# Threshold attention and hash routing: quarter products and sums in PSUM for the experts

## The chip, the cores and the metric

The kernel runs on one core of a Trainium2 chip. Its metric is the device time of one launch in microseconds. Five engines work from queues of their own: TensorE (PE, with its weight loads listed as PEld), VectorE (DVE), ScalarE (ACT), GpSimd (POOL) and SyncE (SP, which only issues DMAs here). All matrices are float32. SBUF holds 128 partitions; PSUM, into which TensorE writes, is used here as tiles of 128 x 2 x 512 floats.

## The reference

```
scores = q @ k^T / sqrt(64)               # 8 batches x 8 heads, 576 x 576
scores = where(scores >= rowmax - tau, scores, -1e9)
attn   = softmax(scores) @ v              # 8 x 8 x 576 x 64
x      = attn as rows                     # 4608 tokens x 512
expert = token_id * 2654435761 % 8        # one of 8 for each token
out    = relu(x @ w1[expert]) @ w2[expert]     # w1 512 x 1024, w2 1024 x 512
```

## The kernel before, in words

The first 500 us or so are attention: pairs of heads, one after the other, with the routing (each token's slot among the tokens of its expert) worked out beside it and the rows of x scattered to DRAM. The change does not touch that part. Around 500 us it goes over into the expert part; everything below is about that.

**Experts.** The experts are sorted by size and get room for 544 tokens (e = 0), 576 (e = 1 to 4) and 600 (e = 5 to 7). Tokens stand along the free axis: x^T is held as 128 x 4 x tokens (`xT_bufs`, two of them), h as 128 x 8 x tokens (`h_0`), the result as 128 x 4 x tokens (`oT`). Layer 1 is h = relu(w1^T x^T), layer 2 is oT = w2^T h. Each is cut into 2 x 2 blocks: the weight's a11, a12, a21, a22 and the tokens' b11, b12, b21, b22, each with half the contraction and half the outputs or half the tokens.

**Seven products.** `seven` (L926) multiplies the blocks with Winograd's form of Strassen's method, seven products for eight. In the product's notation, with sums s1 to s4 of a and t1 to t4 of b (`left` L863, `right` L869; four DVE adds each, in `sums_w1`, `sums_x`, `sums_w2`, `sums_h`):

```
p1 = a11 b11;   u2 = p1 + s2 t2;   u3 = u2 + s3 t3;   u4 = u2 + s1 t1
c11 = p1 + a12 b21;   c21 = u3 + a22 t4;   c22 = u3 + s1 t1;   c12 = u4 + s4 b22
```

Every product is an accumulation of its own in one of four PSUM tiles, taken in turn by `bank2` (L851) from two pools of two. ACT copies p1 into SBUF (L951); DVE makes u2, u3, u4 in SBUF (`halves`) and c11 to c22 (adds, L861; subtractions L858). In layer 1 ACT then applies the ReLU in place (L948). Layer 1 runs in two groups g of 256 outputs each, a product being 2 x 2 calls of matmul (L941); layer 2 is one group with 2 x 4 calls. A call is as wide as half the tokens: 272, 288 or 300 columns, and 240 in layer 2 of e = 7, whose last 120 tokens are done by `last_tile` (L983). The weights of w2 are read with a stride of four columns ("dealt"), except for e = 7. Layer 1 of expert 0 is done as plain products, in part during attention (`early_h`, `late_h`, L632 and L652, with `fill` placing matmuls in gaps).

**Order.** Nothing here is planned by a scheduler. The order of the calls in the code (`manual_schedule`, L1069 to L1122) is the order in each engine's queue, and each engine runs its queue in order; semaphores make it wait for others. The side work of an expert is handed out after each product by `side1` (in layer 1) and `side2` (in layer 2):

- `sums_w2(e)`, `sums_h(e)` in layer 1; `sums_w1(e+1)`, `sums_x(e+1)` in layer 2, on DVE;
- `put_squares(e, i)` (L1024): DVE transposes oT by squares of 32 x 32 into `o_q`, then POOL writes 10 (i = 0, step 3 of layer 2) or 9 (i = 1, step 0 of the next expert) blocks of rows to `out` by indirect DMA;
- `fetch(e+2)` (L1045, step 2 of layer 2): five indirect DMAs on POOL bring rows of x into `xg`;
- `turn_x(e+1)` (L1052): five DVE transposes xg into `xq` (in layer 1, steps 3 to 5), then `move`: 16 DMAs issued by SP, xq into the other xT;
- `load_w1(e+2)` (step 4 of layer 2) and `load_w2(e+2)` (after it): 2 MB each, issued by SP, into a pool of two buffers each.

The end is `put_out` (L997: PE transposes, copies, row writes of the last expert) and `last_tile`.

Of the kernel before, what the change touches and what calls it, by code (L numbers as in the profile page):

```python
# [20 lines left out]
def kernel(  # L21
# [94 lines left out]
    w_tiles = {}  # L116
# [15 lines left out]
    def load_w1(e):  # L132
        w1_sb = w_pool.tile([P, CO, F], FP32, name="w1_sb")
        nc.sync.dma_start(out=w1_sb[:],
                          in_=w1[bass.ds(expert_at(e), 1)].rearrange("o (c p) f -> p (o c) f", p=P))
        w_tiles[e, 1] = w1_sb
# [690 lines left out]
    with tc.tile_pool(name="m_x", bufs=1) as m_x, \  # L827
         tc.tile_pool(name="m_o", bufs=3) as m_o, \
# [9 lines left out]
        o_end = m_x.tile([P, DIN], FP32, name="o_end")  # L838
        mark = m_x.tile([P, 1], FP32, name="mark")
        w1_s = m_s.tile([P, 3, C2, F2], FP32, name="w1_s")  # L840
        CH = CAP // 2
        x_s = m_s.tile([P, 3, C2, CH], FP32, name="x_s")
        w2_s = m_s.tile([P, 3, FH, D2], FP32, name="w2_s")
        h_s = m_s.tile([P, 3, FH, CH], FP32, name="h_s")
        halves = [m_s.tile([P, 2, CH], FP32, name=n) for n in ("p1", "u2", "u3", "u4")]
# [3 lines left out]
        turn = [0]  # L849

        def bank2():  # L851
            turn[0] ^= 1
            if turn[0]:
                return ps_sc.tile([P, 2, 512], FP32, name="sc")
            return ps_m.tile([P, 2, 512], FP32, name="bank2")
# [31 lines left out]
        def w2_sums(e):  # L887
            t = triple(w2_s, 0, FH)
            return t if e == E - 1 else [dealt(x, C2) for x in t]
# [19 lines left out]
        def sums_w2(e):  # L909
            s1 = None  # L910
            if e == E - 1:
                spare = w_pool.tile([P, CO, F], FP32, name="w1_sb")
                s1 = w_tiles["s1"] = spare[:, :, 0:D2]
            return left(*w2_blocks(e, w_tiles[e, 2]), w2_sums(e), s1)
# [11 lines left out]
        def seven(a, a_s, b, b_s, m0, outs, relu, after):  # L926

            (a11, a12, s1, a22), (s2, s3, s4) = a, a_s
            (b11, t1, b21, b22), (t2, t3, t4) = b, b_s
            c11, c12, c21, c22 = outs  # L930
            n_k, width, dealt_out = a11.shape[1], b11.shape[2], len(a11.shape) == 4
            p1, u2, u3, u4 = (t[:, :, 0:width] for t in halves)

            def product(x, y):
                ps = bank2()
                for i in range(2):
                    c0 = m0 + P * i
                    for c in range(n_k):
                        lhsT = (x[:, c, :, i] if dealt_out else
                                x[:, c, c0:c0 + P])  # L940
                        nc.tensor.matmul(ps[:, i, 0:width], lhsT=lhsT, rhs=y[:, c],  # L941
                                         start=c == 0, stop=c == n_k - 1)
                return ps[:, :, 0:width]

            def out(c, ps, u, step):
                add(c, ps, u)()
                if relu:
                    nc.scalar.activation(c, c, AF.Relu)  # L948
                after(step)

            nc.scalar.copy(p1, product(a11, b11))  # L951
            out(c11, product(a12, b21), p1, 0)
            add(u2, product(s2, t2), p1)()
            after(1)
            add(u3, product(s3, t3), u2)()
            after(2)
            out(c21, product(a22, t4), u3, 3)
            k5 = product(s1, t1)
            add(u4, k5, u2)()
            out(c22, k5, u3, 4)  # L960
            out(c12, product(s4, b22), u4, 5)

        def layer1(e, side):

            w, half = w_tiles.pop((e, 1)), caps[e] // 2
            for g in range(NG):
                outs = [h_0[:, FH * i + 2 * g:FH * i + 2 * g + 2, half * k:half * k + half]
                        for i in range(2) for k in range(2)]
                seven(w1_blocks(w), triple(w1_s, 0, C2), x_blocks(e), triple(x_s, 0, C2, half), 2 * P * g,
                      outs, True, lambda step: side(g, step))  # L970

        def layer2(e, side):
# [5 lines left out]
            if e == E - 1:  # L978
                a[2] = w_tiles["s1"]
            seven(a, w2_sums(e), h_blocks(0, FH, half),  # L980
                  triple(h_s, 0, FH, half), 0, outs, False, side)

        def last_tile(middle):  # L983

            w, o_sb, idx = w_tiles[E - 1, 2], o_end, gidx[:, KT - 1:KT]
# [11 lines left out]
        def put_out(e, *groups):  # L997
# [14 lines left out]
            for tr, kts in zip(trs, groups):  # L1012
                for i, kt in enumerate(kts):
                    rows = rows_of(kt)
                    o_sb = m_o.tile([P, DIN], FP32, name="o_sb")
# [53 lines left out]
        with tc.manual_schedule():  # L1069
            run(sums_w2(0), 4)  # L1070
            fill(18)
            late_h(lambda fo: (ps_sc.tile([P, 2, 512], FP32, name="sc") if fo in (2, 4) else
                               ps_m.tile([P, 2, 512], FP32, name="bank2")))
# [3 lines left out]
        with tc.manual_schedule():  # L1077
            for e in range(E):
# [3 lines left out]
                if e > 0:  # L1082
                    w2_work, h_work = sums_w2(e), sums_h(e, 0, 2)

                    def side1(g, step):
                        if g == 0:
                            run(w2_work)
                            if step == 0:
                                put_squares(e - 1, 1)
                        else:  # L1090
                            run(h_work)
                        if step > 2:
                            run(turns, 1 if g == 0 else 2)
# [3 lines left out]
                x_work = (sums_w1(e + 1) + sums_x(e + 1)) if more else []  # L1097

                def side2(step):
                    if step == 0:  # L1100
                        run(turns, len(turns))
                    else:
                        run(x_work, 2)
# [4 lines left out]
                    if more and step == 3:  # L1108
# [88 lines left out]
```

## Time and profile before

| | |
|---|---|
| device time, three runs | 931.68, 934.79, 939.22 us (median 934.79) |
| the profiled execution's own time | 931.3 us |
| its span | 929.7 us |
| granted TensorE clock, mean | 0.996 |
| PE busy | 909.8 us (98%) |
| PEld busy | 662.0 us |
| DVE busy | 757.5 us (81%) |
| ACT busy | 457.3 us |
| POOL busy | 403.7 us |

The profile is one execution on the chip. A busy time counts the time in which an engine had an instruction running; waits and the issue of DMAs are not in it. Weight loads of TensorE are listed apart, since they run beside its matmuls. Lines of the timeline give the start and length in us, the engine, the line of the code, the operation, output<-inputs by the program's names, the shape and how many instructions in a row; what stands in brackets is the idle time before and what ended it. Lines of the waits give the waiting engine's output and line, whom it waited for, the sum in us, how often, and the longest.

### The profile page before, as it was taken

To read this page: it belongs to the slowest core of one execution; us is meant where nothing else is said; L and a number is where in the kernel's file an instruction comes from. 1 tells how busy PE (TensorE), PEld (TensorE's weight loads), DVE (VectorE), ACT (ScalarE), POOL (GpSimd) and SP (SyncE) were. 2 spreads that over 40 slices of the span, in tenths; PEclk is the share of its full clock that TensorE was granted. 3 is DMA by queue.
4 is the path that set the end of the run, shared out by engine and by line. 5 is a ranking of instruction groups with operands and counts; after the bars stand their busy time and mean duration, and the time that the engine had idled before them with its cause. 6 is when DMAs were issued, how large, how long until landed. Compare 5 with 4: busy or idle time off the path is not lost.

```text
span 929.7 us, 20725 instructions
## 1 busy us (share of the span) xinstructions
PE 909.8 (98%) x7495; PEld 662.0 (71%) x7495; DVE 757.5 (81%) x1654; ACT 457.3 (49%) x741; POOL 403.7 (43%) x528
## 2 busy tenths in 40 slices
PE   7999999999999999999999999999999999999996
PEld 4666666656666566665678888788887978878785
DVE  7999999999999999999955776767668676777551
ACT  6888888888888898888812010110201021020110
POOL 4232432456666623455423370724527073440702
PEclk9999999999999999999999999999999999999999
DMA  7354463554545668743101745364372536412101
GB/s 175 92 148 118 109 152 93 136 131 103 123 105 153 159 165 214 216 107 88 30 25 51 237 131 158 133 173 141 95 223 75 164 133 165 157 34 50 48 3 55
DMA packets 114775, 113.11 MB, mean 122 GB/s; under 512 B 32475, under 2 KB 89315, under 8 KB 114672
## 3 DMA queue, kind: packets, MB, share of 16 engines
q1 hardware_dynamic: 105168, 92.64, 37.0%
q0 software_dynamic: 9072, 18.91, 7.0%
q8 instruction: 61, 1.00, 0.4%
q14 instruction: 42, 0.34, 0.1%
q10 hardware_dynamic: 432, 0.21, 0.1%
HBM read 81.99 MB, written 21.44 MB: 111 GB/s over the span
## 4 chain that ended last, share of the span: by engine, by line
PE 65%; issue 21%; POOL 7%; DVE 3%; ACT 2%; DMA 1%; another core or an unknown queue 1%; POOLq 0%; SPq 0%; DVEq 0%; ACTq 0%
PE av L313 18%; PE sc L235 15%; PE tr L282 11%; PE sc L941 9%; PE bank L941 8%; POOL out_dram L1036 6%; PE sc L640 2%; PE av L282 1%; POOL xg L119 1%; ACT w L260 1%; DVE ns L246 1%; DVE w L271 1%; ACT wT_b L303 1%; ACT wT_a L303 0%
## 5 line engine op out<-in xcount | busy, mean ns | idle before, releaser
L260 ACT ACTIVATE w<-ns,nmx 128x576 f32<-128x576 f32 x288 | 220.5, 777 | 28.8 <-DVE ns L246 27.8
L271 DVE SCALAR_TENSOR_TENSOR w<-ns,thr,w 128x576 f32<-128x576 f32 x288 | 225.8, 816 | 0.0
L1036 POOL DMA_INDIRECT out_dram<-o_q,qidx x127 | 138.1, 1087 | 191.7 <-DVE o_q L1028 153.1
L246 DVE TENSOR_SCALAR_CACHE_REDUCE ns<-sc 128x576 f32<-128x576 f32 x288 | 205.6, 747 | 8.1 <-PE sc L235 7.4
L253 POOL TENSOR_SCALAR thr<-nmx,drop 128x2 f32<-128x2 f32 (+1 forms) x160 | 104.4, 653 | 187.3 <-DVE ns L246 177.6
L235 PE MATMUL sc<-k_sb,q 64*128 64x288 f32 (+1 forms) x1280 | 179.2, 423 | 1.0 <-DVE drop L704 0.7
L282 PEld LDWEIGHTS tr<-ident,w 64*128 64x128 f32 x2624 | 106.0, 138 | 95.4 <-ACT wT_b L303 32.4
L282 PE MATMUL tr<-ident,w 64*128 64x64 f32 x2624 | 139.5, 231 | 6.0 <-ACT wT_b L303 2.6
L948 ACT ACTIVATE h<-h 128x576 f32<-128x576 f32 (+1 forms) x56 | 38.7, 693 | 164.8 <-DVE h L861 126.1
L235 PEld LDWEIGHTS sc<-k_sb,q 64*128 64x128 f32 (+1 forms) x1280 | 93.0, 177 | 23.2 <-DVE ns L246 9.4
L313 PE MATMUL av<-wT_a,v 128*64 128x320 f32 (+1 forms) x704 | 100.6, 418 | 0.2
L303 ACT COPY wT_a<-tr 128x512 f32<-128x512 f32 (+1 forms) x128 | 81.7, 638 | 20.7 <-PE tr L282 20.2
L303 ACT COPY wT_b<-tr 128x512 f32<-128x512 f32 (+1 forms) x128 | 81.4, 636 | 17.1 <-PE tr L282 11.2
L313 PE MATMUL av<-wT_b,v 128*64 128x256 f32 x640 | 83.2, 389 | 0.0
L313 PEld LDWEIGHTS av<-wT_a,v 128*64 128x64 f32 x704 | 43.8, 137 | 29.3 <-DVE xm L352 0.7
L951 ACT COPY p<-bank 128x576 f32<-128x576 f32 (+2 forms) x11 | 7.0, 633 | 99.5 <-PE bank L941 72.5
L313 PEld LDWEIGHTS av<-wT_b,v 128*64 128x64 f32 x640 | 40.2, 136 | 18.8 <-issue 0.7
L542 POOL DMA_INDIRECT slot_scratch<-tok,slot_i x36 | 45.0, 1251 | 9.4 <-issue 7.6
L941 PE MATMUL bank<-h,w_sb 128*128 128x288 f32 (+3 forms) x192 | 48.1, 404 | 0.0
L941 PE MATMUL sc<-h,w_sb 128*128 128x288 f32 (+3 forms) x192 | 47.7, 401 | 0.0
L941 PEld LDWEIGHTS bank<-h,w_sb 128*128 128x128 f32 x192 | 46.6, 300 | 0.5
L941 PEld LDWEIGHTS sc<-h,w_sb 128*128 128x128 f32 x192 | 45.9, 289 | 0.6
(197 smaller groups left out, 1303.7 us busy)
## 6 DMA issues: line engine op xcount, KB each, us to landing
w_sb<-in_moe_w_dram SPq DMA_DIRECT2D x16, 2048.0 KB
q<-in_q_dram SPq DMA_DIRECT2D x62, 288.0 KB
v<-in_v_dram SPq DMA_DIRECT2D x32, 256.0 KB
x_scratch<-xm SPq DMA_DIRECT2D x32, 256.0 KB
xT<-xq SPq DMA_DIRECT2D x84, 80.0 KB
k_sb<-in_k_dram SPq DMA_DIRECT2D x31, 144.0 KB
k_sb<-in_k_dram SPq DMA_DIRECT2D x32, 112.0 KB
x_scratch<-xg SPq DMA_DIRECT2D x9, 256.0 KB
```

What stands on the lines that cost most here:

```text
L235: nc.tensor.matmul(sc[out_rows, i, 0:S2], lhsT=q_sb[rows, h, q0:q1], rhs=k_sb[rows, h], start=True, stop=True)
L246: nc.vector.tensor_scalar(out=ns[:].rearrange("p (i s) -> p i s", i=2), in0=sc[:, :, 0:S2], scalar1=-1.0, scalar2=None, op0=ALU.mult, op1= ...
L253: nc.gpsimd.tensor_scalar(out=thr[:, 0:j + 1], in0=stats[n][0][:, 0:j + 1], scalar1=drop[:], scalar2=None, op0=ALU.add)
L260: nc.scalar.activation(w, nss[n, j][:], AF.Exp, bias=stats[n][0][:, j:j + 1], scale=-1.0)
L271: nc.vector.scalar_tensor_tensor(out=w, in0=nss.pop((n, j))[:], scalar=stats[n][1][:, j:j + 1], in1=w, op0=ALU.is_le, op1=ALU.mult, accum_ ...
L282: nc.tensor.transpose(dst[:, r, 64 * c:64 * c + 64], src[rows, c0:c0 + P], ident[rows, rows])
L303: nc.scalar.copy(dst, tr[:, :, 0:64 * n_c].rearrange("p r (c q) -> p r c q", c=n_c))
L313: nc.tensor.matmul(av[64 * j:64 * j + 64, g, c0:c1], lhsT=v_sb[:, c, 64 * j:64 * j + 64], rhs=wT[g][:, i, c0:c1], start=(c == 0), stop=stop)
L542: nc.gpsimd.indirect_dma_start(out=slot_dram[c % 2][:, :], out_offset=bass.IndirectOffsetOnAxis(ap=slot_i[:, c:c + 1], axis=0), in_=tok[:, ...
L941: nc.tensor.matmul(ps[:, i, 0:width], lhsT=lhsT, rhs=y[:, c], start=c == 0, stop=c == n_k - 1)
L948: nc.scalar.activation(c, c, AF.Relu)
L1036: inst = nc.gpsimd.indirect_dma_start(out=rows[:, :], out_offset=bass.IndirectOffsetOnAxis(ap=idx, axis=0), in_=o_sb, in_offset=None, boun ...
```

## The change

Two things are done, and the side work is dealt out anew.

**Sums in PSUM.** `seven` becomes the class `Seven`. p1 stays in its PSUM tile and s2 t2, s3 t3 and a22 t4 are accumulated on top of it (`start=False`), so that the tile holds p1, u2, u3 and c21 one after the other; ACT copies p1 and u2 (and u3 or s1 t1, `mid`) into SBUF in between, since other results need them. s1 t1 and s4 b22 share another tile; DVE adds u2 to it for c12. The tiles no longer rotate: each step names its `banks[0..3]`, and the pool `m_o` and the tile `o_end` go (`xg_bufs` take their place).

**Quarters.** a12 b21, one of the seven products, is itself done by seven products of quarters (class `Quarters`): in layer 1 once for both groups together, in layer 2 once. Every quarter product is two calls of matmul, half as wide as the others (144 or 150 columns, and 120 in layer 2 of e = 7). Their own sums are made by DVE (`inner_w`, `inner_b`); w2's quarter is first copied by ACT into dense order (`copy_quarters`). What they give is written to the places of c11, and p1 is added there later (`c11`). Expert 0's layer 2 keeps the plain product (`second`).

**Side work.** For e > 1 the five transposes of `turn_x` and its move stand at steps 1 and 2 of layer 1; `put_squares(e, 0)` stands in the middle of the last product of layer 2; for e = 1 `put_squares(0, 0)` stands at step 0, `put_squares(0, 1)` at step 4 and the transposes at steps 5 to 9. A one-element ACT copy into `mark_w` at step 1 of layer 2 reads w1 of expert e, whose buffer `load_w1(e+2)` fills. The fourth sum of w2 of expert 0 is made inside its layer 2 (`w2_first`).

```diff
+        def late_tile(fo):
+            if fo in (2, 4):
                 return ps_sc.tile([P, 2, 512], FP32, name="sc")
             return ps_m.tile([P, 2, 512], FP32, name="bank2")
...
+        def bank2():
+            turn[0] += 1
+            return banks[(turn[0] - 1) % 4]
...
+        def products(ps, x, y, start, mid=None):
+            for i, lhsTs in enumerate(x):
+                for c, lhsT in enumerate(lhsTs):
+                    nc.tensor.matmul(ps[:, i], lhsT=lhsT, rhs=y[:, c], start=start and c == 0,
+                                     stop=c == len(lhsTs) - 1, skip_group_check=not start)
+                if i == 0 and mid:
+                    mid()
...
+            def out(self, c, ps, u):
                 add(c, ps, u)()
+                if self.relu:
+                    self.later.append(lambda: nc.scalar.activation(c, c, AF.Relu))
...
+            def first(self):
+                products(self.x, self.a[0], self.b[0], True)
+            def keep_p1(self):
+                nc.scalar.copy(self.p1, self.x)
+            def second(self, y):
+                y = y[:, :, 0:self.x.shape[2]]
+                products(y, self.a[1], self.b[2], True)
+                self.out(self.outs[0], y, self.p1)
+            def u2_sum(self):
+                products(self.x, self.a[4], self.b[4], False)
+                nc.scalar.copy(self.u2, self.x)
+            def s1_t1(self, keep):
+                products(self.z, self.a[2], self.b[1], True)
+                if keep:
+                    nc.scalar.copy(self.mid, self.z)
+            def u3_sum(self, keep):
+                products(self.x, self.a[5], self.b[5], False)
+                if keep:
+                    nc.scalar.copy(self.mid, self.x)
+            def c21(self):
+                products(self.x, self.a[3], self.b[6], False)
+                if self.relu:
+                    nc.scalar.activation(self.outs[2], self.x, AF.Relu)
+                else:
+                    nc.scalar.copy(self.outs[2], self.x)
+            def c12(self, mid=None):
+                products(self.z, self.a[6], self.b[3], False, mid)
+                self.out(self.outs[1], self.z, self.u2)
+            def c22(self, ps):
+                self.out(self.outs[3], ps, self.mid)
+            def c11(self, p1):
+                self.out(self.outs[0], p1, self.outs[0])
+        class Quarters:
...
+            def p1_p2(self):
+                products(self.x, self.a[0], self.b[0], True)
+                nc.scalar.copy(self.p1, self.x)
+                products(self.y, self.a[1], self.b[2], True)
+            def c11(self):
+                add(self.outs[0], self.y, self.p1)()
+            def p5_u2(self):
+                products(self.z, self.a[2], self.b[1], True)
+                nc.scalar.copy(self.p5, self.z)
+                products(self.x, self.a[4], self.b[4], False)
+                nc.scalar.copy(self.u2, self.x)
+            def c12_c22(self):
+                products(self.z, self.a[6], self.b[3], False)
+                add(self.outs[1], self.z, self.u2)()
+                products(self.x, self.a[5], self.b[5], False)
+                add(self.outs[3], self.x, self.p5)()
+            def c21(self):
+                products(self.x, self.a[3], self.b[6], False)
+                nc.scalar.copy(self.outs[2], self.x)
...
+        def copy_quarters(e):
+            w = w2_blocks(e, w_tiles[e, 2])[1]
+            nc.scalar.copy(w2_q[:].rearrange("p (i j) k m -> p i (j k) m", i=2),
+                           w.rearrange("p k m i -> p i k m"))
...
+            q = quarters_of(e, 1, *banks[1:])
+            g0, g1 = group(0, banks[0], banks[2]), group(1, banks[1], banks[3])
+            w_tiles.pop((e, 1))
+            g0.first()
+            g0.keep_p1()
+            side(0)
+            q.p1_p2()
+            q.c11()
+            g0.u2_sum()
+            side(1)
+            q.p5_u2()
+            g0.s1_t1(True)
+            side(2)
+            q.c12_c22()
+            side(3)
+            g0.u3_sum(False)
+            q.c21()
+            g0.c22(g0.x)
+            side(4)
+            g0.c12()
+            g0.c11(g0.p1)
+            g1.first()
+            g0.relus()
+            side(5)
+            g1.c11(g1.x)
+            g1.relus()
+            g0.c21()
+            side(6)
+            g1.u2_sum()
+            side(7)
+            g1.s1_t1(True)
+            side(8)
+            g1.u3_sum(False)
+            side(9)
+            g1.c22(g1.x)
+            g1.c12()
+            g1.relus()
+            side(10)
+            g1.c21()
...
+            o = Seven(a, w2_sums(e), h_blocks(0, FH, half), triple(h_s, 0, FH, half), 0, outs,
+                      False, *((banks[0], banks[1]) if e else (banks[3], banks[2])))
+            o.first()
+            o.keep_p1()
+            if e == 0:
+                o.second(banks[0])
+                run(w2_first)
+                side(0)
+                o.u2_sum()
+                side(1)
+                o.s1_t1(True)
+                side(2)
+                o.u3_sum(False)
+                o.c22(o.x)
+                side(3)
+                o.c12()
+                side(4)
+                o.c21()
+                return
+            q = quarters_of(e, 2, *(banks[i][:, 0:1] for i in (2, 3, 3)))
+            q.p1_p2()
+            q.c11()
+            run(inner_b(second_blocks(e, 2)[1]), 4)
+            o.u2_sum()
+            q.p5_u2()
+            side(0)
+            o.u3_sum(True)
+            side(1)
+            q.c12_c22()
+            o.s1_t1(False)
+            side(2)
+            q.c21()
+            o.c11(o.p1)
+            o.c22(o.z)
+            o.c21()
+            side(3)
+            o.c12(lambda: side(4))
...
+            w2_first = sums_w2(0)
+            run(w2_first, 3)
             fill(18)
+            late_h(late_tile)
+            for _ in range(2):
+                banks += [ps_sc.tile([P, 2, 512], FP32, name="sc"),
+                          ps_m.tile([P, 2, 512], FP32, name="bank2")]
...
+                    a, b = second_blocks(e, 2)
                     w2_work, h_work = sums_w2(e), sums_h(e, 0, 2)
+                    w2_work += inner_w(a, None if more else w_tiles["s1_q"])
+                    def side1(step):
+                        if step == 0 and e == 1:
+                            put_squares(0, 0)
+                        if step == (0 if e > 1 else 4):
+                            put_squares(e - 1, 1)
+                        if step == 2 and more:
+                            copy_quarters(e)
+                        run(turns, ((0, 2, 4, 0, 0, 0, 0, 0, 0, 0, 0) if e > 1 else
+                                    (0, 0, 0, 0, 0, 1, 1, 1, 1, 2, 0))[step])
+                        run(w2_work, ((0, 0, 0, 1, 1, 0, 1, 1, 1, 1, 0) if e > 1 else
+                                      (0, 1, 2, 0, 0, 0, 1, 0, 1, 1, 0))[step])
+                        run(h_work, 2 if step in (8, 9) else 0)
 
                     layer1(e, side1)
                     run(sums_h(e, 2, FH), 4)
+                    run(w2_work, len(w2_work))
+                x_work = []
+                if more:
+                    a, b = second_blocks(e + 1, 1)
+                    x_work = [sums_w1(e + 1), sums_x(e + 1), inner_w(a), inner_b(b)]
+                    if e == 0:
+                        x_work[1:3] = x_work[2:0:-1]
+                    x_work = sum(x_work, [])
 
                 def side2(step):
                     if step == 0:
                         run(turns, len(turns))
+                    run(x_work, ((1, 2, 3, 10, 0) if e else (2, 2, 0, 4, 8))[step])
+                    if step == 1 and e + 2 < E:
+                        nc.scalar.copy(mark_w[0:1, :], last_w1[e][0:1, 0, 0:1])
                     if step == 2 and e + 2 < E:
                         fetch(e + 2)
                     if step == 4 and e + 2 < E:
                         load_w1(e + 2)
+                    if more and e and step == 4:
                         put_squares(e, 0)
...
```

Lines that go (`seven` whole, the old `side1` and `side2`) are left out of this cut; they stand in the kernel above.

## The prediction

> **What bounds the kernel now.** I read the page's busy table first (TensorE, PE, 909.8 of 929.7 us), then the timeline of PE in the expert part, then PE's waits, then the groups by shape. These are the first products of experts 1 to 7 and the first product of layer 2 of expert 7 (start, length, engine, line, output<-inputs, count):
>
> ```profile
> 526.98 2.10 PE L941 MATMUL bank<-xT,w_sb 128*128 128x288 f32 x8
> ...
> 583.29 2.10 PE L941 MATMUL sc<-xT,w_sb 128*128 128x288 f32 x8
> ...
> 637.61 2.10 PE L941 MATMUL bank<-xT,w_sb 128*128 128x288 f32 x8
> ...
> 692.48 2.10 PE L941 MATMUL sc<-xT,w_sb 128*128 128x288 f32 x8
> ...
> 746.80 2.18 PE L941 MATMUL bank<-xT,w_sb 128*128 128x300 f32 x8
> ...
> 803.36 2.18 PE L941 MATMUL sc<-xT,w_sb 128*128 128x300 f32 x8
> ...
> 861.29 2.18 PE L941 MATMUL bank<-xT,w_sb 128*128 128x300 f32 x8
> ...
> 890.91 3.40 PE L941 MATMUL bank<-h,w_sb 128*128 128x240 f32 x16
> ```
>
> A call of matmul leaves two records, so a product of layer 1 (2 x 2 calls) is 8 records and one of layer 2 is 16. Undisturbed products follow each other by 1.94 us (583.29 to 585.23), 0.2425 us a record of 288 columns; 300 columns take 0.2525 (2.02 / 8), 240 take 0.2025 (3.24 / 16). An expert has 112 calls, 224 records: 54.32 us at 288, 56.56 at 300. The starts above give 56.31, 54.32, 54.87, 54.32, 56.56, 57.93 for experts 1 to 6, and 29.62 for layer 1 of expert 7 (112 records: 28.28). So PE is at its pace, and beyond it lost 1.99 + 0 + 0.55 + 0 + 0 + 1.37 + 1.34 = **5.25 us**. Who made it wait (waits of its loads, 526 to 911 us):
>
> ```profile
> PEld bank L941 <- DVE h_s L858: 2.8, 2, 2.1
> PEld sc L941 <- ACT p L951: 1.1, 1, 1.1
> PEld bank L941 <- ACT p L951: 1.0, 1, 1.0
> ```
>
> Sums of h that came late (experts 1 and 3) and the copy of p1 (6 and 7). In expert 1 the cause is odd:
>
> ```profile
> 552.20 2.10 PE L941 MATMUL sc<-xT,w_s 128*128 128x288 f32 x8
> ...
> 560.84 0.76 DVE L861 TENSOR_TENSOR h<-sc,u 128x576 f32<-128x576 f32 x1 [4.50 <-remote]
> ```
>
> The product was there at 554.3, VectorE (DVE) was free at 556.3, the add began at 560.84. Such late starts of up to 1.5 us, rarely more, stand in other experts too, on DVE and ScalarE (ACT), nearly all while GpSimd (POOL) issues indirect DMAs; I have no cause for them.
>
> **What the Trainium skill says.** "TensorE: Matmul & The Clock Gate", Back-to-back issue gap: at full clock a matmul follows the last by columns / 2.4 ns + 2.5 ns. The records agree if a float32 record takes two cycles a column: 288 / 1.2 + 2.5 = 242.5 ns. The same page, LDWEIGHTS: a load takes columns / 1.2, 107 ns for 128; the trace records 190 ns (308 for the dealt w2), but overlapped. "PSUM — Partial Sum Buffer", The four PSUM rules: a matmul that doesn't open a group adds to what TensorE wrote there before, and reads by other engines don't change that; so a sum in PSUM costs PE nothing. The same page, PSUM bank collisions: two engines may not be on one bank and quadrant together; so the next addend must wait until a copy has read the last sum. No run yet shows the last two.
>
> **The change, part by part.** Narrow records first. The trace has one narrow stream, the last tile's:
>
> ```profile
> L990 PEld LDWEIGHTS sc<-w_sb,h x16: 183/183/183, 920.1 to 921.9; 128*120 128x120 f32 x16
> L990 PE MATMUL sc<-w_sb,h x16: 272/273/273, 920.4 to 922.0; 128*120 128x128 f32 x16
> ```
>
> 16 starts in 1.6 us, 0.107 a record, as columns / 1.2 + 2.5 has it (0.109), though each load is recorded at 183 ns. So I price 144 columns at 0.1225, 150 at 0.1275, 120 at 0.1025. The other end is 0.190, a load's own record, if loads of 128 columns could not overlap.
>
> (1) a12 b21 was 16 records in each layer; it becomes 7 products of 4 narrow ones, 28. Experts 1-4: 2 x (16 x 0.2425 - 28 x 0.1225) = 0.90 each, 3.60; experts 5 and 6: 2 x (4.04 - 3.57) = 0.94 each, 1.88; expert 7: 0.47 + (3.24 - 2.87) = 0.84. Sum **-6.3 us**, all on PE's path. Expert 0 runs layer 2 with `second`, as before.
>
> (2) Sums in PSUM. The adds of u2, u3, u4 and of c21 leave DVE: 12 x 0.75 = 9.0 us an expert. DVE gains 6 adds of half size and 16 quarter sums; a fit of its rows (480: 0.653, 576: 0.753, 1024: 1.214) gives 0.16 + 1.03 ns an element: 6 x 0.46 + 8 x 0.42 + 4 x 0.31 + 4 x 0.46 = 9.2. DVE's load stays (40.1 of 54.3 us in expert 2). ACT gains u2, mid, some c21 (about 7 x 0.63), 8 quarter copies (0.40) and the copy of w2's quarter (1024 elements, about 1.0): +9 us on 7.2, with room. No cost by itself; without that room each copy would stand in PE's way in full.
>
> (3) The waits that this adds. PE may not add to an accumulator until its copy is done, and everything on PE is queued behind. Copies begin 0.24 us after the next product does (640.43 - 0.64 = 639.79 against 639.55), last 0.64, and PE resumed 0.06 after a copy when it had waited (826.79 to 826.85), with 0.1 lost in restarting loads. That is 0.94 to 1.05 us. The cover at three places an expert (`first` to `u2_sum` in layer 1; `first` to `u2_sum` and `u2_sum` to `u3_sum` in layer 2) is two quarter products, 8 x 0.1225 = 0.98. Between nothing and 0.2; I take 0.07 x 3 x 7 = **+1.5**.
>
> (4) DVE's reads before PE may reuse a bank. Laying the new order out at these durations, from an expert's first product: q.c22's add ends at 9.4, its bank is wanted at 10.7; g1.c11 16.0 against 17.0; g1.c22 23.8 against 24.7; t2 of layer 2 at 28.8 against 31.5. Before, four banks taken in turn gave an add nearly two products. POOL issues rows (19 x 1.29 us) and gathers through most of that stretch, where the late starts stand. Nothing if these go, 1.5 us an expert if each hits; I take 0.4 x 7 = **+2.8**.
>
> (5) The old stalls: p1 of group 1 is no longer copied, nothing waits for u2-u4 on DVE, and c12 comes before c21, so sums of h begin a product earlier. I let all go: **-5.25**. What is late next is (4).
>
> (6) Squares and moves. Five transposes (0.69 us each) go from the end of layer 1 to steps 1 and 2, and with them 16 SP DMAs (10.3 to 11 us of issue), past the loads of w1 and w2 that SP issues later, and the five gathers on POOL (1.3 us each), which still come after 19 row writes. At these steps they end 7.2 us into the expert, before DVE's next add at 8.5. The half-row writes (9 on POOL) move into the last product. The w1 load waits for the marker on ACT, some 41 us in, and is wanted about 50 us later. DMA is free elsewhere (share 0.47): 0 us; if a gather came late, DVE would hold, and PE with it.
>
> (7) Start. Expert 0's first product now goes to the last bank of the pool of two, which `late_h`'s last add frees at 501.94 (501.22 + 0.72) instead of one long free: PE was there at 501.02; **+1.1** with restart. Then the fourth sum of w2 (1.22) stands before the squares, so the move lands near 527.2 instead of 524.8, while expert 1 would begin at 527.8: hidden, barely. The end (put_out, last tile) keeps its parts.
>
> Sum: -6.3 - 5.25 + 1.5 + 2.8 + 1.1 = **-6.2 us** against the profiled execution's own 931.3: 925.1. That one was 3.5 below the median of 934.79; from the median I forecast **928.6**. About 1% (9.3 us) is what a measurement of this kernel can tell from no change.
>
> **Rivals.** (A) The forecast, 925 to 932: chance 0.50. (B) The new waits cost next to nothing: -6.3 - 5.25 + 1 to 2, near 924. For it: copies just fit, experts 2, 4 and 5 ran without a lost slot. Chance 0.22. (C) **PE waits for its own accumulators.** Mechanism: ACT's and DVE's late starts, which four rotating banks absorbed, land on PE. Place: g1.c11 and g1.c22 in layer 1, the three copies of (3). Price: two late starts of 1.2 us and three of 0.2 are 3 us an expert, 21 in all: -6.3 - 5.25 + 1.1 + 21 = +10.6, 945. It decides from 10.5 / 7 = 1.5 us an expert on, where the gain is gone. For it: late starts of 1 to 1.5 us stand in most experts at 13 to 30 us; against: DVE in back-to-back work showed none, and now has more of that there. Chance 0.23, from level to slower. (D) Narrow records at the load's 0.190: 392 x 0.0675 = +26 us, 955. Against it the last tile's stream. Chance 0.05. Whether the calls are cut can't fail: the count is in the code.
>
> **Numbers.** Faster by over 1% (below 925.4): most of B and the edge of A, 0.26. Slower by over 1% (above 944.1): half of C and D, 0.16. Within: 0.58. The range 922 to 942 leaves out D, the upper part of C, and the best of B.
>
> **What would show it.** Records of 144 columns should start 0.1225 us apart, and an undisturbed expert take 53.4 us at 288 columns instead of 54.32. PE's waits should name ACT copies (p, u) with a few hundredths each and DVE's adds into h; if they name adds with over 1 us an expert, C is right. The first product of expert 0 should start near 502.1. DVE's busy time stays. What makes it wrong: waits on accumulators of another size than (3) and (4), or late starts that vanish with the other order of DMAs.

## The result and the profile after

The changed kernel took **1042.42 us** (median of 1037.40 to 1056.61) beside 937.0 us for the kernel before, a ratio of **1.1115, 95% interval 1.103 to 1.1201**. Repeated in another measurement it took 1031.08 beside 932.18 (1.0987, 1.0911 to 1.1064). In a third it took **914.97 beside 919.36 (0.9951, 0.9934 to 0.9967)**: it gained. What divides these measurements is in the profile, and it is the subject of all that follows. I read the repeat (profiled execution 1033.4 us, span 1031.8), since the first one's profiled execution, 1056.61 us, was the longest of its four.

The busy table of the repeat, with PE's row and the granted clock:

```profile
span 1031.8 us, 21304 instructions
...
PE 926.2 (90%) x7663; PEld 681.0 (66%) x7663; DVE 756.0 (73%) x1720; ACT 514.8 (50%) x854; POOL 401.1 (39%) x528
...
PE   8999999999999999999999939959669759779797
...
PEclk9999999999999999999999969989879879889999
```

PE is no longer busy throughout: from the 24th slice on (593 us, in expert 2) every expert has a hole, and the granted clock falls beside it. The waits of PE from 520 us on (waiting output, for whom, sum in us, times, longest):

```profile
PE bank L940 <- issue: 48.4, 7, 14.9
PE bank L940 <- ACT h L1043: 35.4, 4, 13.0
PE bank L940 <- DVE h L867: 3.5, 2, 1.9
PE sc L940 <- issue: 1.6, 1, 1.6
```

Where they name a releaser, it is a copy or an add that reads an accumulator, as the third rival of the prediction has it. For half of the time they name none ("issue"), and one of these waits is 15 us long. Expert 4 shows both kinds from inside. These are its lines in the timeline of all engines (start, length, engine, line, operation, output<-inputs, idle time before and what ended it):

```profile
732.59 12.18 SPq L1273 DMA_DIRECT2D xT<-xq  x16
733.14 0.98 POOL L1245 DMA_INDIRECT out_dram<-o_q,qidx  x1 [0.30 <-issue]
...
733.72 0.65 PE L940 MATMUL bank<-bi_s,wi_s 128*128 128x144 f32 x4
...
734.21 2.10 PE L940 MATMUL sc<-x_s,w_s 128*128 128x288 f32 x8
...
744.82 0.46 DVE L867 TENSOR_TENSOR h<-bank,q_p 128x288 f32<-128x288 f32 x1 [7.41 <-remote]
745.20 1.22 DVE L864 TENSOR_TENSOR w_s<-w_sb 128x1024 f32<-128x1024 f32 x1
745.34 1.33 PE L940 MATMUL bank<-bi_s,w_sb 128*128 128x144 f32 x4 [9.02 <-issue]
...
746.46 3.57 PE L940 MATMUL sc<-xT,w_s 128*128 128x288 f32 x8
...
755.43 1.00 POOL L119 DMA_INDIRECT xg<-x_scratch,gidx_x  x1 [0.30 <-issue]
759.59 0.40 ACT L1043 COPY h<-bank 128x288 f32<-128x288 f32 x1 [23.24 <-remote]
759.60 0.76 DVE L867 TENSOR_TENSOR h<-sc,u 128x576 f32<-128x576 f32 x1 [13.19 <-remote]
760.04 2.29 PE L940 MATMUL bank<-xT,w_sb 128*128 128x288 f32 x4 [10.02 <-ACT h L1043]
```

The quarter product of 733.72 has its last record by 734.4; the add that reads it (744.82) starts 10.4 us later, with DVE idle for the last 7.4 of them. The product of 734.21 ends by 736.3; the add that reads it starts at 759.60. "Remote" means that a semaphore for which the instruction waits rose just then, too long after the record that raises it. Both adds wait for TensorE's semaphore (the second for an ACT copy too, over by 734.42). A sum that waits for no semaphore of TensorE (745.20) starts at once. So what is late is **TensorE's completion signal**, not DVE or ACT. The trace also holds times at which the semaphore rose, paired here in order with the ends of the records that raise it:

```
product of expert 4             record's end   signal    later by
u2 of the quarters                 731.45      731.47     0.01 us
c22 of the quarters                734.37      744.80    10.43
u3                                 736.31      759.51    23.20
c21 of the quarters                746.66      759.57    12.91
c12                                750.03      759.66     9.63
first product of group 1           763.73      763.74     0.01
```

Two products are left out: s1 t1 (0.37 us late), and c12 of the quarters, whose rise the trace lacks. It lacks 21 of TensorE's 971 rises in this profile, so the pairs rest on the instructions that wait as well: the adds of 744.82 and 759.60 and the copy of 759.59 start within 0.1 us of their signals.

The Trainium skill, "Perfetto Trace Analysis", Tensor Engine Instruction (MATMUL, LD_WEIGHTS), says that a matmul's reported end is an estimate and that the semaphore is raised only once PSUM has acknowledged the writes. Here the estimate fits within 0.02 us on either side of the hold, and the last three held signals come 0.06 to 0.09 us apart; a trace can't say where in between they were held. It does say when: GpSimd's indirect DMAs run without a break from 726.66 to 756.43, SP issues the move from 732.59 to 744.77, and the last signals come 3.1 us after GpSimd's last.

The same expert in the measurement that gained:

```profile
688.92 10.71 SPq L1273 DMA_DIRECT2D xT<-xq  x16
...
690.06 0.65 PE L940 MATMUL bank<-bi_s,wi_s 128*128 128x144 f32 x4
...
690.55 2.10 PE L940 MATMUL sc<-x_s,w_s 128*128 128x288 f32 x8
690.75 0.46 DVE L867 TENSOR_TENSOR h<-bank,q_p 128x288 f32<-128x288 f32 x1
692.49 0.65 PE L940 MATMUL bank<-bi_s,w_sb 128*128 128x144 f32 x4
692.76 0.76 DVE L867 TENSOR_TENSOR h<-sc,u 128x576 f32<-128x576 f32 x1 [0.42 <-PE sc L940]
```

The same order of work, and both adds start within 0.3 us of their product. This expert took 53.76 us (681.77 to 735.53), the one above 76.80 (725.43 to 802.23).

**The sum of the loss.** Without late signals the span is 913.9 us. In the repeat, PE reached layer 2 of expert 0 at 500.04 instead of 494.36 us, 5.7 us lost in attention, which the change does not touch and where the kernel before loses about as much (500.46 to 501.02 against 494.35). From then on PE's records leave gaps of 94.6 us in 22 places, and records at half pace cost 15.9: 913.9 + 5.7 + 94.6 + 15.9 = 1030.1 of 1031.8. The half pace is the clock. The skill's "TensorE: Matmul & The Clock Gate", What's actually happening, says that after an idle window of some 3.4 us the array runs at half clock until it has been busy for one; the trace agrees: after the wait of 9.02 us the 8 records of 746.46 took 3.57 us instead of 2.10, and the granted clock was 0.5 for 89 us of the experts' time.

### The profile page after: what moved, and what is told of

Read it like the earlier page. It is cut to its first block, busy times and chain, and to the rows that moved or that the text cites. A ratio compares the mean times of both kernels' runs of the same rounds, so it can differ in the third digit from the quotient of the medians.

```text
span 1055.0 us, 21304 instructions
## 1 busy us (share of the span) xinstructions
PE 936.8 (89%) x7663; PEld 686.9 (65%) x7663; DVE 755.5 (72%) x1720; ACT 514.4 (49%) x854; POOL 399.9 (38%) x528
## 4 chain that ended last, share of the span: by engine, by line
PE 58%; issue 29%; POOL 6%; ACT 3%; another core or an unknown queue 2%; DVE 1%; DMA 1%; POOLq 0%; SPq 0%; ACTq 0%; DVEq 0%
PE av L313 16%; PE sc L235 13%; PE tr L282 10%; PE sc L940 8%; PE bank L940 7%; POOL out_dram L1245 5%; PE sc L640 2%; PE av L282 1%; POOL xg L119 1%; ACT w L260 1%; ACT wT_b L303 1%; ACT wT_a L303 1%; PE bank L658 0%; PE sc L658 0%
## 5 line engine op out<-in xcount | busy, mean ns | idle before, releaser
L1245 POOL DMA_INDIRECT out_dram<-o_q,qidx x127 | 131.3, 1034 | 320.0 <-DVE o_q L1237 267.3
L940 PE MATMUL bank<-xT,w_sb 128*128 128x288 f32 (+3 forms) x168 | 49.4, 439 | 26.8 <-ACT h L1043 26.8
L940 PE MATMUL bank<-h,w_sb 128*128 128x288 f32 (+4 forms) x248 | 62.0, 402 | 0.0
L940 PEld LDWEIGHTS bank<-xT,w_sb 128*128 128x128 f32 x168 | 35.1, 223 | 39.5 <-ACT h L1043 29.1
L940 PEld LDWEIGHTS bank<-h,w_sb 128*128 128x128 f32 x248 | 58.7, 290 | 0.5
L940 PE MATMUL sc<-h_s,w_s 128*128 128x288 f32 (+2 forms) x224 | 56.6, 406 | 0.0
L964 ACT ACTIVATE h<-h 128x576 f32<-128x576 f32 (+1 forms) x42 | 29.0, 692 | 53.6 <-DVE h L867 48.4
L940 PE MATMUL bank<-x_s,w_s 128*128 128x288 f32 (+1 forms) x112 | 35.2, 464 | 18.2 <-issue 15.2
```

The source lines that it names most:

```text
L940: nc.tensor.matmul(ps[:, i], lhsT=lhsT, rhs=y[:, c], start=start and c == 0, stop=c == len(lhsTs) - 1, skip_group_check=not start)
L964: self.later.append(lambda: nc.scalar.activation(c, c, AF.Relu))
L1245: inst = nc.gpsimd.indirect_dma_start(out=rows[:, :], out_offset=bass.IndirectOffsetOnAxis(ap=idx, axis=0), in_=o_sb, in_offset=None, boun ...
```

## The experiments

Ten measurements held the kernel before and some other kernel side by side. In four of them TensorE's signals were late, and the kernel before took 931.4 to 937.5 us; in the other six none was more than 0.3 us late, and it took 918.6 to 919.4. I call them *late* and *prompt* measurements; no execution of the kernel before took less than 927.6 us in a late one or more than 920.8 in a prompt one. Which it would be could not be chosen, and I found nothing in the kernels that decides it. The theories that the expectations name: **theory 1**, SP's move beside GpSimd's row writes holds the signals; **theory 2**, the many short quarter products do; **theory 3**, the signals were always late and the new accumulators have no slack for it; **theory 4**, added after the first four runs, late signals belong to the measurement, or to the chip, and not to the change.

**The move late, the quarters left out, the move early in the kernel before, no row writes.** The first four, a prompt measurement (before: 918.87). The move late:

```diff
-                        run(turns, ((0, 2, 4, 0, 0, 0, 0, 0, 0, 0, 0) if e > 1 else
-                                    (0, 0, 0, 0, 0, 1, 1, 1, 1, 2, 0))[step])
+                        run(turns, (0, 0, 0, 0, 0, 1, 1, 1, 1, 1, 0)[step])
```

> The changed kernel, with the five transposes of turn_x at steps 5 to 9 of layer 1 in every expert and the move (16 SP DMAs) at step 0 of layer 2, after the gathers. Theory 1 (TensorE's completion signals are held up while SP's move and GpSimd's row writes are issued at once): the waits of 6 to 15 us an expert go, about 930 to 950 us. Theory 2 (the many short quarter products are held up by GpSimd's issue alone): 1020 to 1050, as with the change. Theory 3 (each delay that the kernel before also had now lands on TensorE, since its accumulators have no slack): 960 to 1000.

Measured: 916.74, ratio 0.9977 (0.9969 to 0.9985), no signal late. By the trace this move doesn't come after the gathers, as the expectation has it: in expert 2 it starts 22.7 us into the expert instead of 7.2 and ends at 605.87, beside the last of GpSimd's indirect DMAs (606.02). "Late" means this below. The quarters left out:

```diff
             side(0)
-            q.p1_p2()
-            q.c11()
+            g0.second(banks[1])
             g0.u2_sum()
...
-            g0.c11(g0.p1)
             g1.first()
+            g1.keep_p1()
...
+            g1.second(banks[3])
             g1.u2_sum()
...
-            q.p1_p2()
-            q.c11()
-            run(inner_b(second_blocks(e, 2)[1]), 4)
+            o.second(banks[2])
             o.u2_sum()
```

> The changed kernel, but a12 b21 as one plain product in both layers (no quarters), everything else, the early transposes and move too, as changed. Theory 1: still 1020 to 1050, since the move and the row writes still meet. Theory 2: 935 to 960. Theory 3: about as slow as with the change, 1000 to 1050.

Measured: 925.68, 1.0076 (1.0059 to 1.0093). (Here the fourth sum of w2 lies over a12 before the plain product of layer 2 reads it, so that product has another operand; instructions and shapes are those meant.) Without late signals it says something else that is worth having. PE's waits from 510 to 910 us and the place in expert 1:

```profile
PE sc L940 <- ACT u L982: 5.4, 7, 0.8
```

```profile
554.08 4.04 PE L940 MATMUL sc<-h_s,w_s 128*128 128x288 f32 x16
558.90 4.15 PE L940 MATMUL sc<-h_s,w_s 128*128 128x288 f32 x16 [0.78 <-ACT u L982]
```

From 554.08 the next product is due at 557.96 and comes at 558.90: 0.94 us. That is the copy of u2 between two accumulations into one tile when no quarter product lies between. With the quarters, the same place costs 0.02 to 0.1. The move early in the kernel before:

```diff
-                        if step > 2:
+                        if e > 1:
+                            run(turns, {(0, 1): 2, (0, 2): 4}.get((g, step), 0))
+                        elif step > 2:
                             run(turns, 1 if g == 0 else 2)
```

> The kernel before with one part of the change: for e > 1 two transposes of turn_x at step 1 and three and the move at step 2 of the first group of layer 1. Theory 1: completion signals come 5 to 20 us late here too, so 990 to 1040. Theory 2: within 1% of before. Theory 3: signals late but mostly absorbed by four rotating banks, 940 to 965.

Measured: 921.25, 1.0026 (1.0016 to 1.0035). No row writes:

```diff
-            for s in range(s0, s1):
+            for s in range(s0, s1 if e == 0 else s0):
                 put_rows(o_q[i][:, s - s0].rearrange("p a c -> p (a c)"), qidx[:, e, s:s + 1],
```

> The changed kernel without the row writes of put_squares for experts 1 to 6 (their results are not stored); the DVE transposes into o_q, the gathers and the move stay. Theory 1: without row writes beside the move no signal is over 1 us late, about 915 to 930. Theory 2: the same. Theory 3: the same. If instead the move alone holds up the signals, 1000 to 1040.

Measured: 914.77, 0.9956 (0.994 to 0.9972). None of the theories could show itself here: with prompt signals the four lie within 1.3% of each other.

**The changed kernel again, and the kernel before for its profile.**

> The changed kernel as it is, since the first four experiments showed no completion signal of TensorE later than 0.3 us and a time before of 919 us instead of 937. Theory 1 and 3: if signals are late again, 1020 to 1050. New theory 4 (the late signals are a condition of the first measurement and not of the change): none late, 912 to 918 us beside 919 before.

> The kernel before, for its profile beside that of the changed one. Theory 4: no late signal, 919 us, TensorE's lost time in experts 1 to 7 under 2 us instead of 5.25. Theories 1 and 3: late signals of 1 to 8 us in every expert as in its first profile.

> The changed kernel with a12 b21 as one plain product in both layers and the fourth sum of w2 after it. All theories, if no signal is late: the changed kernel's time plus 6.3 us for the longer products, less what the quarters' waits cost. If signals are late: theory 2 under 960, theories 1 and 3 about 1040.

A late measurement (before: 932.18). The changed kernel 1031.08, read above. The kernel before 931.95: its signals were late by up to 7 us too, and its experts 1 to 6 lost 5.3 us in all. The version without quarters, now with the fourth sum made after a12 is read, 1014.29 (1.0913, 1.0858 to 1.0968). **Theory 2 falls**: without a single quarter product the loss is 82 us instead of 99.

**Does the changed kernel bring the late signals about?**

> The changed kernel on another chip, beside the version with the late move. Theory 4 (whether signals are late belongs to the chip; with none late the change gains a little): 912 to 918 if the kernel before takes 919 here, 1020 to 1050 if it takes 927 or more. If the late signals come from the changed kernel itself, it is over 1000 here too.

> The changed kernel with the late move on the same chip. Where the kernel before takes 919: 917, as twice before. Where it takes 927 or more: theory 1 (move beside row writes) 925 to 950; theory 3 (no slack in the accumulators) 970 to 1030.

A prompt measurement: 914.97 (0.9951, 0.9934 to 0.9967) and 916.72. So the changed kernel doesn't bring them about: theory 4 holds as far as that. Its other half, that the chip decides, doesn't hold by the numbers on record: chips 4 (the repeat, and this measurement) and 11 each had a late and a prompt one. The late move was also run three other times and the early move in the kernel before two other times:

> The changed kernel with the transposes at steps 5 to 9 and the move at step 0 of layer 2, again, for a measurement in which TensorE's completion signals are late (it then shows in the time before, 927 us or more instead of 919). If they are: theory 1 (SP's move beside GpSimd's row writes is what holds the signals for 10 to 23 us) 925 to 950; theory 3 (accumulators without slack suffice) 970 to 1030. If they are not: 917 again.

> The kernel before with the transposes and the move early, again, likewise. If signals are late: theory 1 970 to 1030, since a hold of over 8 us outlasts four banks; theory 3 under 950. If they are not: 921 again.

> The changed kernel with the late move once more, for a measurement with late signals (the kernel before then takes 927 us or more). There: theory 1 (SP's move beside GpSimd's row writes makes the holds long) 925 to 950; theory 3 (accumulators without slack suffice) 970 to 1030. Without late signals 917.

> The kernel before with the early move once more, likewise. With late signals: theory 1 970 to 1030; theory 3 under 950. Without: 921.

> The kernel before, for its profile where no signal is late (919 us): TensorE loses under 1.5 us in experts 1 to 7 instead of 5.25, so the changed kernel's gain there is that of the narrow records less its own waits. Where signals are late: 927 us or more, as in its first profile.

> The changed kernel with the late move. Where signals are late: theory 1 925 to 950, theory 3 970 to 1030. Where none is: 917.

All prompt: 916.59, 916.78 and 916.70 for the late move, 921.22 and 921.40 for the early one, 920.14 for the kernel before. Its profile (span 918.6) has experts of 55.07, 54.31, 54.32, 54.32, 56.56, 56.56 us: it lost 0.75 us in all of them, not 5.25.

**Both orders in one profile.** Since a late measurement could not be had at will, the next kernel holds both orders:

```diff
-                        run(turns, (0, 0, 0, 0, 0, 1, 1, 1, 1, 1, 0)[step])
+                        run(turns, ((0, 0, 0, 0, 0, 1, 1, 1, 1, 1, 0) if e in (1, 2, 5) else (0, 2, 4, 0, 0, 0, 0, 0, 0, 0, 0))[step])
```

> The changed kernel with the late move in experts 1, 2 and 5 and the early move in experts 3, 4 and 6, so that one profile holds both. Where signals are late: theory 1 expects 54 to 58 us for experts 2 and 5 and 68 to 80 for expert 4; theory 3 (accumulators without slack) expects experts 2 and 5 to be as long as with the early move, 70 to 80. Where none is late: 53.8 to 54.4 for 2 to 4 and 55.9 to 56.3 for 5 and 6, about 916 us in all.

A late measurement: 1032.44 beside 937.52 (1.1013, 1.0894 to 1.1133). First products of experts 1 to 7, and the waits of PE over 2.5 us in experts 1 to 5:

```profile
529.11 2.10 PE L940 MATMUL sc<-xT,w_sb 128*128 128x288 f32 x8
...
558.65 4.21 PE L940 MATMUL bank<-x_s,w_s 128*128 128x288 f32 x8 [8.42 <-issue]
...
567.87 3.74 PE L940 MATMUL bank<-xT,w_s 128*128 128x288 f32 x8 [5.01 <-ACT u L987]
...
600.42 2.10 PE L940 MATMUL sc<-xT,w_sb 128*128 128x288 f32 x8
...
618.61 3.90 PE L940 MATMUL bank<-xT,w_sb 128*128 128x288 f32 x8 [2.96 <-ACT h L1043]
...
661.56 2.10 PE L940 MATMUL sc<-xT,w_sb 128*128 128x288 f32 x8
...
682.77 3.38 PE L940 MATMUL bank<-x_s,w_s 128*128 128x288 f32 x8 [4.02 <-DVE h L867]
...
698.93 4.21 PE L940 MATMUL bank<-x_s,w_s 128*128 128x288 f32 x8 [10.32 <-ACT u L982]
...
734.44 2.10 PE L940 MATMUL sc<-xT,w_sb 128*128 128x288 f32 x8
...
757.33 1.33 PE L940 MATMUL bank<-bi_s,w_sb 128*128 128x144 f32 x4 [12.01 <-issue]
...
769.35 3.70 PE L940 MATMUL bank<-xT,w_sb 128*128 128x288 f32 x8 [6.96 <-ACT h L1043]
...
811.55 2.18 PE L940 MATMUL sc<-xT,w_sb 128*128 128x300 f32 x8
...
829.79 3.78 PE L940 MATMUL bank<-xT,w_sb 128*128 128x300 f32 x8 [2.85 <-ACT h L1043]
...
873.94 2.18 PE L940 MATMUL sc<-xT,w_sb 128*128 128x300 f32 x8
...
948.27 2.18 PE L940 MATMUL sc<-xT,w_sb 128*128 128x300 f32 x8
```

Late move: expert 2 took 61.14 us, expert 5 62.39. Early move: experts 3, 4 and 6 took 72.88, 77.11 and 74.33. Neither theory alone says this: between these experts the late move takes away 12 to 16 us, but 6 to 7 stay.

Expert 1 doesn't fit. It has the late move too and took 71.31 us, where the prompt profiles with the late move have 53.81; with the changed kernel's own order, which moves at step 9 there, it took 71.84 in the first measurement and 55.57 in the repeat. Its row writes start later, so that its move (551.02 to 561.64) lies within GpSimd's indirect DMAs (534.37 to 564.54), while the moves of experts 2 and 5 start 4.6 us before the end of theirs. But two signals were held in expert 1 before its move began: of records that ended at 546.35 and 548.29, one rose at 549.53, the other at 557.94. So a hold can begin without a move, against theory 1.

**The same mixture in the kernel before.**

```diff
-                        if step > 2:
+                        if e in (3, 4, 6):
+                            run(turns, {(0, 1): 2, (0, 2): 4}.get((g, step), 0))
+                        elif step > 2:
                             run(turns, 1 if g == 0 else 2)
```

> The kernel before with the early move in experts 3, 4 and 6 and its own order in 1, 2 and 5. Where signals are late: if the early move makes the holds long by itself, signals are 10 to 23 us late in experts 3, 4 and 6 and these take 62 to 75 us, experts 2 and 5 55 to 58; if it takes accumulators without slack as well, experts 3 and 4 stay under 58 and expert 6 under 60. Where none is late: 54.3 to 55.1 for experts 2 to 4, 56.6 to 57.4 for 5 and 6, about 920 us in all.

A prompt measurement, 920.40 (1.0016, 1.0008 to 1.0023). Once more:

> The same mixture in the kernel before once more, for a measurement with late signals: experts 3, 4 and 6 at 62 to 75 us if the early move alone makes the holds long, under 58 and 60 if it takes accumulators without slack as well. Without late signals 920 us again, and the question stays open.

Late this time (before: 931.4): 932.79, ratio 1.001 (0.9995 to 1.0026). First products of experts 2 to 7:

```profile
584.41 2.10 PE L941 MATMUL sc<-xT,w_sb 128*128 128x288 f32 x8
...
638.73 2.10 PE L941 MATMUL bank<-xT,w_sb 128*128 128x288 f32 x8
...
694.90 2.10 PE L941 MATMUL sc<-xT,w_sb 128*128 128x288 f32 x8
...
749.79 2.18 PE L941 MATMUL bank<-xT,w_sb 128*128 128x300 f32 x8
...
806.35 2.19 PE L941 MATMUL sc<-xT,w_sb 128*128 128x300 f32 x8
...
864.23 2.18 PE L941 MATMUL bank<-xT,w_sb 128*128 128x300 f32 x8
```

Early move: experts 3, 4 and 6 took 56.17, 54.89 and 57.88 us; in the prompt run of this kernel 54.90, 54.90 and 56.95. So what late signals added to an expert (late less prompt; for the changed kernel against the profiles with the late move, 54.31 and 56.17, and with the early one, 53.76 and 55.89):

| | late move | early move |
|---|---|---|
| four banks in turn, sums in SBUF (before) | 0.0 (experts 2, 5) | 1.3, 0.0, 0.9 (experts 3, 4, 6) |
| fixed banks, sums in PSUM (after) | 6.8, 6.2 (experts 2, 5) | 19.1, 23.4, 18.4 (experts 3, 4, 6) |

In the kernel before the early move costs little: 0.4 to 0.6 us an expert when signals are prompt, and at most 1.3 more when they are late. In the table the long losses stand where the early move meets the fixed accumulators. That it takes these two, and both, is not shown:

- "Early" is not the same moment in the two kernels: the move starts 14.7 to 15.2 us into the expert in the kernel before and 7.2 us in the changed one.
- The two rows also differ in the quarters and the rest of the side work. The version without quarters clears the quarters alone.
- Experts of one order vary. Expert 1 is one case. In the late profile without quarters, where every expert from 2 on has the early move and the fixed accumulators, experts 2, 4 and 5 lost 16.2 to 17.6 us against its prompt profile, but 3 and 6 only 1.2 and 2.4; in the repeat expert 3 lost 13.5.

What is shown is the step from a late signal to a lost microsecond: PE stands until a copy or an add has read its accumulator, and these stand until TensorE's signal comes.

**What stays open.** Why signals are late in some measurements and in others, of the same kernels, not; how an indirect DMA or the move's issue holds them; and why a hold is longer in the changed kernel. That a hold lengthens because TensorE stands and sends no more signals would fit the table and was not tried. The late move everywhere and the kernel without row writes were never run in a late measurement. One mark of a late measurement is in the traces: of the semaphore rises of TensorE, DVE and ACT together, each late profile lacks 139 to 178 and each prompt one 5 to 19, most of them already in attention. Whether one thing delays the signals and thins the record of them, or the recording has a part in the delay, no run tells.

## Why the prediction was wrong

The time, 1042 us, lies far outside the range. The step that failed is **(4)**, the price of late starts: I put "0.4 x 7" us on it, and in the third rival "two late starts of 1.2 us and three of 0.2", 3 us an expert. Measured, experts 1 to 6 of the repeat lost (427.9 - 326.9) / 6 = 16.8 us each. The mechanism of that rival and its sign were right: copies and adds that start late hold up PE, which needs its accumulator again. Its size and its places were not.

- **Size.** I read lateness from the idle time of DVE and ACT, 1.5 us. By TensorE's semaphore, signals in the same profile came up to 6.5 us late: in expert 1 for a record that ended at 554.30 (signal 560.82), in expert 6 for one of 819.68 (826.05). There an add has nearly two products of room, and most of the delay passed while DVE had other work. I also took a late start for a delay of a fixed length and multiplied. In the changed kernel PE stops within a product or two of a held signal, and the next signals are held as well, up to 23.2 us.
- **Places.** Of the 88.9 us of waits above, the places that the rival names had 5.1. The product after the quarters' c22, whose add (4) does list, had 24.8. The most, 50.3, fell on the first product of group 1, which waits until ACT has copied the quarters' c21 out of the same tile, and 8.7 on a wait for the copy of group 1's u2 in expert 3. No step of the prediction priced a wait for these two copies.

The odd line of the prediction's own profile, an add that started 4.50 us late in expert 1 "<-remote", was this. I wrote that I had no cause for it and then priced it. The times of the semaphore's rises were in the same trace.

- **(1), narrow records: right.** Four records of 144 columns start 0.49 us apart from the next four (528.31 to 528.80 in the prompt profile), 0.1225 a record. The skill's "TensorE: Matmul & The Clock Gate", Back-to-back issue gap, gives the formula that I used for a matmul by itself and not for a stream; in this case streams keep to it as well, at two cycles a column.
- **(2), sums in PSUM: right.** DVE was busy 755.5 us (757.5 before), and the copies fitted where signals were prompt.
- **(3), copies between accumulations: right in mechanism, 0.31 us an expert instead of 0.21.** The four products of 16 records after a quarter product are 3.90, 3.96, 3.99 and 3.98 us apart from what follows instead of 3.88. Uncovered, the price was put at 0.94 to 1.05; without quarters it measured 0.94.
- **(5), the old stalls: wrong in cause.** I let 5.25 us go because the sums of h begin a product earlier. They were late signals, the copy of p1 in expert 6 too (826.13): the kernel before loses 0.75 us where none is late.
- **(6), the move at 0 us: wrong where signals are late** (12 to 16 us an expert between experts 2 to 6 of the mixed kernel), right to 0.6 us where they are prompt (expert 2: 53.76 with the early move, 54.31 with the late one, which is the dearer).
- **(7), 1.1 us at the start of expert 0: didn't occur** (494.36 against 494.35 us).

Where signals are prompt the steps hold together: -6.3 of narrow records, +2.2 of (3), -0.75 of stalls is -4.9 us; the spans are 913.9 and 918.6, -4.7. That the forecast of -6.2 us lies near this is luck: it counted 5.25 us of stalls, of which 0.75 exist there, and 3.9 us of (4) and (7), of which nothing does.

## What to carry to other kernels

A wait that is hidden today has no price in the profile: before taking away buffers that rotate, ask how late the signals behind it can come, and what the engine does if it must stand still for them. The idle time of the waiting engine understates that while it has other work; the rise of the semaphore doesn't. An idle time that ends "remote" is worth following to its semaphore before it is priced. And a change that gains half a per cent by using up slack can lose ten where conditions differ, so repeat the measurement before trusting either number.

## What was not expected of the hardware

- TensorE's completion signals rose up to 23 us after the end of their records, in four of ten measurements, and in the experts only for records that ended while GpSimd issued indirect DMAs one after the other or within 0.5 us after. In each of the 19 experts that lost over 10 us, the last held signal came within 4 us after GpSimd's last, in most of them with the one before it 0.06 to 0.10 us ahead. Where PE waited for DVE or ACT, their signals were not held: PE went on at 745.34, when the add of 744.82 was just over.
- A hold needs no move beside it (expert 7 of the kernel before; experts 2 and 5 of the mixed kernel, whose signals were up to 5.4 us late before their move began). In the changed kernel holds began within 2 us of the move's first DMA in experts 2 and 4 of the repeat (588.80 and 732.59 against records that ended at 590.6 and 733.4).
- In the repeat, after waits of 3.8 us and more the clock was granted at 0.5, and the next full product of eight records took 3.0 to 4.4 us instead of 2.1 to 2.2; after waits of under 2 us it was not. This cost 15.9 us beside 94.6 of waiting.
